# Gating two chunks a period sooner, and another order of the late block, in a retention + top-1 expert kernel on one Trainium2 core

## The chip, the core and the metric

The kernel runs on one core of a Trainium2 chip. Its engines work side by side and wait for each other by semaphores: TensorE (PE, with PEld for its weight loads), VectorE (DVE), ScalarE (ACT), GpSimd (POOL) and SyncE (SP, which issues most DMAs here; GpSimd issues the indirect ones). The metric is the device time of one execution in microseconds.

## What is computed

A retention (a decaying linear attention) over 4 batches of 768 positions, 8 heads of 64, gives 3072 rows of 512 numbers. Each row then goes through the one of 8 experts that its gate chooses, and is weighted by that gate's probability.

```python
for t in range(S):
    state = gamma * state + einsum('bhd,bhe->bhde', k[:, :, t], v[:, :, t])
    y[:, :, t] = scale * einsum('bhd,bhde->bhe', q[:, :, t], state)
...
logits = x @ w_gate
expert_idx = np.argmax(logits, axis=1)
...
for e in range(E):
    mask = expert_idx == e
    out[mask] = gate_w[mask, None] * (np.maximum(x[mask] @ w1[e], 0.0) @ w2[e])
```

## The kernel before

**Retention.** The 3072 rows are 24 chunks of 128, taken in 12 periods n = 0 to 11 of two chunks each (the loop `for n in range(last + 1)`). A period runs scores, state updates (`update` copies the state to a tile `ub` on ScalarE), outputs (`carry` reads `ub`, `output`), and `evict` writes the result xT. One period later `rows` transposes it to rows (`xrow`), and `logits` and `finish_logits` make gate logits.

**Gating.** Chunks are gated in groups, by the table `GROUPS` of (first chunk, count). A group is gated in the period after its last chunk: `choose` (VectorE: argmax, one-hot `EA`, shifted logits), `soft` (ScalarE: exp), `rank` (TensorE: small matmuls that count, for each row, the rows of the same expert ahead of it; one matmul for each earlier group's total among them), `slots` (VectorE: each row's slot, `KEY`), `weights`, `label` (ScalarE: weight and token number into `xrow`), `advance`. In the table of before, chunks 18 to 21 are one group, gated behind the loop; 22 and 23 follow.

**Scatter.** GpSimd sends each chunk's rows by an indirect DMA to their slots in `x_sorted` in DRAM, sorted by expert (`send_apart`, line 840). Between two sends stands `pause()`, a small operation (`idle`, line 201). After the last chunk come pads of zeros behind the regions.

**Expert 0's first 256 rows ("early").** Expert 0 is the class with the fewest rows among the first six chunks. Its first rows are read before the last period, and its matmuls (`early_pieces`, run by `fill`) fill TensorE from period 11 on, while the last chunks are gated and sent.

**Late block.** `late_block` takes up to 128 more rows of expert 0 (`xhl1`, read by SyncE as `xg1` after the last send). Its first layer is `hidden(i, part)` for weight halves i = 0, 1; ScalarE applies Relu (`hs`); `turned(i)` transposes on TensorE, ScalarE casts the high half of `hT` and VectorE subtracts for its low half (fp32 is carried as two fp32r numbers, high and low, so each product is three matmuls); `result(i, part)` is the second layer. In the same code the other engines prepare expert 1: its rows, read by SyncE into `buf`, are turned (VectorE), cast to `xh` (ScalarE) and subtracted to `xl` (VectorE) in four pieces by `prep(j, ...)`; the first part of its weights is split into `whi` (ScalarE) and `wlo` (VectorE) in two halves by `split(1, 0, i)`; `marks(1)` reads slot numbers. `weigh` (VectorE) scales the early results `Z0`, and `put_slices` (GpSimd) sends them to the output, eight indirect DMAs. The same buffers (tag "w", 11 of them, in turn) hold `Z0` and all weight halves.

**Experts 1 to 7** follow with all their rows each: eight column blocks of the first layer, then four of the second; weights are fetched by SyncE into two `raw` buffers, and split as they come free.

All this stands under a manual schedule: each engine runs its instructions in the order in which the code issues them.

Of the kernel before, what the change touches and what calls it, by code (L numbers as in the profile page):

```python
# [10 lines left out]
F32 = mybir.dt.float32  # L11
# [32 lines left out]
MAXB = CMAX32 // 32  # L44
WARM = 8
FILL = (1, 3, 4)
GROUPS = ((0, 6), (6, 6), (12, 4), (16, 2), (18, 4), (22, 2))
FULL = 18
BEHIND = {3: (0, 1), 4: (2, 3), 5: (4, 5), 6: (6, 7), 7: (10, 11), 8: (12, 13)}
AMID = {7: (8, 9)}  # L50
# [57 lines left out]
def retention_moe(ctx, tc, front, qkv, w1, w2, first_rows, second_rows, out):  # L108
# [112 lines left out]
    with ExitStack() as actx:  # L221
# [17 lines left out]
        def load(g, part=slice(0, 4)):  # L239
            if g not in qs:  # L240
                early = AHEAD <= g < FIRST or g in MID
                qs[g] = (wp.tile([P, 4, DM], F32, name="qkv_w", tag="w", bufs=11) if early else
                         ld.tile([P, 4, DM], F32, name="qkv_t", tag="ld"))
            nc.sync.dma_start(out=qs[g][:, part],
                              in_=front[2 * g + part.start // 2 - (g > 0)] if g <= AHEAD else qkv[g - AHEAD - 1])
# [22 lines left out]
        def bank(i, name, shape=(P, NP, C)):  # L268
            return ps_s.tile(list(shape), F32, name=name, tag=f"s{i}")
# [88 lines left out]
        def send_apart(chunks, between=pause):  # L358
            for i, g in enumerate(chunks):
                if i:  # L360
                    between()
                send_rows(g)
# [42 lines left out]
        def gating(i):  # L405
# [31 lines left out]
                nc.scalar.activation(out=ex[:, :, 0:E], in_=v["sh"], func=AF.Exp)  # L437

            def rank():
                pf = v["pf"] = bank(2, "pf", (P, NB, E)) if i < 3 else ps_1.tile([P, NB, E], F32, name="pf", tag="U" if i == 4 else "misc")  # L440
                nc.tensor.matmul(out=pf[:, 0:w, :], lhsT=us, rhs=Eb, start=True, stop=False, skip_group_check=True)
                for part in [run] + tots:
                    nc.tensor.matmul(out=pf, lhsT=ones, rhs=part.unsqueeze(1).broadcast_to([P, NB, E]),
                                     start=False, stop=False, skip_group_check=True)
                for n in range(NB - 1):
                    nc.tensor.matmul(out=pf[:, n + 1:, :], lhsT=ones,
                                     rhs=Eb[:, n:n + 1, :].broadcast_to([P, NB - 1 - n, E]),
                                     start=False, stop=(n == NB - 2), skip_group_check=True)
# [87 lines left out]
        def mark_early():  # L536
            xg0 = first["xg"]
            index, weight = slot_marks[0]
            empty = gsm.tile([P, NJ0], F32, name="empty0")
            nc.vector.tensor_tensor(out=empty, in0=k_("slot")[:, 0:NJ0], in1=s0.broadcast_to([P, NJ0]), op=ALU.is_ge)  # L540
            nc.vector.tensor_scalar(out=mask0, in0=empty, scalar1=float(BIG), scalar2=k_("quad"),
                                    op0=ALU.mult, op1=ALU.add)
            nc.vector.scalar_tensor_tensor(out=index[:, 0:NJ0], in0=xg0.bitcast(I32)[:, :, P], scalar=4 * ROWS,
                                           in1=mask0, op0=ALU.bitwise_and, op1=ALU.bitwise_or)
            nc.vector.tensor_copy(out=weight[:, 0:NJ0], in_=xg0[:, :, P + 1:P + 2])
# [60 lines left out]
        for n in range(last + 1):  # L606
# [95 lines left out]
            for g in (a, b):  # L702
                if FIRST <= g < NCH - AHEAD - len(MID):
                    load(g + AHEAD + len(MID))
                if g in fetches:
                    fetch(0, fetches[g])
                for i in LATER.get(g, ()):
                    load(i)
        mark_early()

        s = stages[4]
        fill(FILL[0])
        rows(2 * last, "U", ps_1)
        logits(last)
# [3 lines left out]
        s["rank"]()  # L718
        for name in ("slots", "weights", "advance", "label"):
            s[name]()  # L720
        send_apart(range(18, 22))
        finish_logits(last)
        final = gating(5)
        final["choose"]()
        fill(FILL[2])
        final["soft"]()
# [205 lines left out]
def moe_main(ctx, tc, wparts, fetch, split, xhl1, Z0, ident, buf, xg, fetch_rows, expert_at, held7, mask7, slot_marks, natural, overflow,  # L932
# [112 lines left out]
    def put_slices(e, j):  # L1045
        pause()
        scatter_rows(tc, out_slices, sidx[e][:, j:j + 1], Zs[e][:, j].rearrange("p k r -> p (k r)"), "rows")

    def late_block():

        hs = [yp.tile([P, DM], F32, name="hs", tag="yo") for _ in range(2)]
        hT = yp.tile([P, 2, KF, P], F32R, name="hT", tag="Z")
        hn = {}

        def hidden(i, part):
            whi, wlo = wparts[0, i]
            if part == 0:
                hn[i] = next(hidden_banks)
            for kd in range(2 * part, 2 * part + 2):
                for n, (a, x) in enumerate(((whi, 0), (wlo, 0), (whi, 1))):  # L1060
                    nc.tensor.matmul(out=hn[i], lhsT=xhl1[:, x, kd, :], rhs=a[:, kd, :],
                                     start=(kd == 0 and n == 0), stop=(kd == KD - 1 and n == 2))
            if part:
                nc.scalar.activation(out=hs[i], in_=hn[i], func=AF.Relu)

        def turned(i):
            t = next(hidden_banks).rearrange("p (j t) -> p j t", j=4)
            for j in range(4):
                nc.tensor.transpose(out=t[:, j, :], in_=hs[i][:, j * P:(j + 1) * P], identity=ident)
            hi, lo = [hT[:, n, 4 * i:4 * i + 4, :] for n in range(2)]  # L1070
            nc.scalar.copy(out=hi, in_=t)
            nc.vector.tensor_tensor(out=lo, in0=t, in1=hi.bitcast(F32), op=ALU.subtract)

        def result(i, part):
            whi, wlo = wparts[0, 2 + i]
            terms = ((whi, 0), (wlo, 0), (whi, 1))
            order = ([(f, n) for f in range(2 * part, 2 * part + 2) for n in range(3)] if i == 0 else
                     [(f, n) for f in range(4) for n in ((0, 1) if part == 0 else (2,))])
            for f, n in order:
                a, h = terms[n]  # L1080
                nc.tensor.matmul(out=pys[0], lhsT=hT[:, h, 4 * i + f, :], rhs=a[:, f, :],
                                 start=(i + f == 0 and n == 0), stop=(i == 1 and f == 3 and n == 2))

        prep = lambda j, *steps: prep_x(1, j, nc.vector, steps)
        for j in range(-(-NJ0 // 4)):
            weigh(0, j)
        for j in range(NJ0):
            put_slices(0, j)
        hidden(0, 0)
        hidden(0, 1)  # L1090
        prep(0, "turn")
        prep(1, "turn")
        prep(0, "high", "low")
        hidden(1, 0)
        turned(0)
        prep(1, "high")
        prep(2, "turn")
        hidden(1, 1)
        prep(1, "low")
        split(1, 0, 0, nc.vector)  # L1100
        result(0, 0)
        turned(1)
        prep(2, "high")
        split(1, 0, 1, nc.vector)
        prep(3, "turn")
        prep(2, "low")
        prep(3, "high", "low")
        marks(1)
        result(0, 1)
        result(1, 0)  # L1110
        result(1, 1)
        put_rows(0, pys[0], 0)

    with tc.manual_schedule():
# [238 lines left out]
```

## Time and profile before

| | us |
|---|---|
| time, median of 3 runs (lowest to highest) | 385.07 (384.97 to 385.78) |
| profiled execution | 385.23 |
| its span, first to last instruction | 383.5 |
| TensorE busy | 373.7 (97%) |
| VectorE busy | 251.6 (66%) |
| GpSimd busy | 263.5 (69%) |
| ScalarE busy | 140.4 (37%) |
| mean granted TensorE clock | 0.995 |

The views are all of one profiled execution, in microseconds from its first instruction. [...] The late block lies at 121 to 138, expert 1 behind it.

### The profile page before, as it was taken

The page shows a single profiled execution, that of the slowest core. Times are in us where ns is not written, and L with a number is a line of the kernel's source. Part 1 is how long each engine was busy: PE and PEld are TensorE (multiplying, and loading weights), DVE is VectorE, ACT ScalarE, POOL GpSimd, SP SyncE. Part 2 cuts the span into 40 slices and gives each one's busy share as a digit, 9 for nine tenths or more (in the row PEclk, how much of TensorE's full clock was granted, in tenths as well). Part 3 has the DMA queues.
Part 4 walks back from the last instruction along what each step waited for, and adds up shares of the span by engine and source line. Part 5 has one row for each costly group of instructions (what it writes and reads, how often), then busy time and mean ns, then how long its engine had stood idle before and what let it go on. Part 6 is the DMA issues. An engine that isn't in the chain of part 4 may idle for free. (4 is left out here: it accounts for less than half of the span.)

```text
span 383.5 us, 8677 instructions
## 1 busy us (share of the span) xinstructions
PE 373.7 (97%) x3272; PEld 350.5 (91%) x3272; DVE 251.6 (66%) x485; ACT 140.4 (37%) x248; POOL 263.5 (69%) x279
## 2 busy tenths in 40 slices
PE   7999999999999799999999999999999999999995
PEld 4888888788999589999999999999999999999984
DVE  3467758875787567877785778576766667676211
ACT  2222344245331446434441453154335416423100
POOL 3751669989380598005999799499759939986874
PEclk9999999999999899999999999999999999999999
DMA  8999999985037879769653773665466547530102
GB/s 305 416 414 420 415 399 419 414 339 170 32 140 149 287 183 252 243 222 249 215 216 78 190 234 141 131 220 159 154 174 194 201 83 233 181 125 17 37 29 76
DMA packets 42030, 82.05 MB, mean 214 GB/s; under 512 B 4267, under 2 KB 17583, under 8 KB 39536
## 3 DMA queue, kind: packets, MB, share of 16 engines
q1 hardware_dynamic: 36656, 67.67, 53.9%
q0 software_dynamic: 5312, 13.49, 9.8%
q8 instruction: 47, 0.77, 0.8%
q14 instruction: 15, 0.12, 0.1%
HBM read 65.80 MB, written 15.82 MB: 213 GB/s over the span
## 5 line engine op out<-in xcount | busy, mean ns | idle before, releaser
L840 POOL DMA_INDIRECT out<-Z,sidx x88 | 101.7, 1155 | 62.2 <-DVE Z L1043 47.4
L146 DVE TENSOR_TENSOR wlo<-raw,whi 128x1024 fp32r<-128x1024 f32 (+1 forms) x63 | 75.4, 1201 | 14.9 <-ACT whi L145 14.7
L201 POOL TENSOR_TENSOR idle<-cs 1x256 bf16<-1x256 f32 x103 | 82.5, 801 | 2.9
L145 ACT CAST whi<-raw 128x1024 fp32r<-128x1024 f32 (+1 forms) x72 | 67.5, 950 | 3.2 <-DMA raw<-w 3.2
L1201 PE MATMUL py<-hh,whi 128*128 128x392 f32 (+4 forms) x192 | 65.9, 343 | 0.0
L1201 PE MATMUL py<-hl,whi 128*128 128x392 f32 (+4 forms) x192 | 65.9, 343 | 0.0
L1201 PE MATMUL py<-hh,wlo 128*128 128x392 f32 (+4 forms) x192 | 65.9, 343 | 0.0
L1176 ACT ACTIVATE hh<-ph 128x452 fp32r<-128x452 f32 (+6 forms) x56 | 28.4, 507 | 76.9 <-PE ph L1169 75.2
L1169 PE MATMUL ph<-xh,whi 128*128 128x392 f32 (+5 forms) x224 | 48.9, 340 | 0.0
L1169 PE MATMUL ph<-xl,whi 128*128 128x392 f32 (+5 forms) x224 | 48.9, 340 | 0.0
L1169 PE MATMUL ph<-xh,wlo 128*128 128x392 f32 (+5 forms) x224 | 48.9, 340 | 0.0
L1177 DVE SCALAR_TENSOR_TENSOR hl<-ph,hh 128x452 fp32r<-128x452 f32 (+6 forms) x56 | 32.1, 574 | 20.8 <-ACT hh L1176 19.9
L1169 PEld LDWEIGHTS ph<-xh,whi 128*128 128x128 f32 x224 | 40.1, 188 | 0.7 <-ACT xh L862 0.5
L1169 PEld LDWEIGHTS ph<-xh,wlo 128*128 128x128 f32 x224 | 40.2, 188 | 0.1
L1169 PEld LDWEIGHTS ph<-xl,whi 128*128 128x128 f32 x224 | 40.2, 188 | 0.1
L1201 PEld LDWEIGHTS py<-hl,whi 128*128 128x128 f32 x192 | 36.1, 188 | 0.2
L1201 PEld LDWEIGHTS py<-hh,wlo 128*128 128x128 f32 x192 | 36.1, 188 | 0.2
L1201 PEld LDWEIGHTS py<-hh,whi 128*128 128x128 f32 x192 | 36.0, 188 | 0.2
L862 ACT CAST xh<-buf 128x512 fp32r<-128x512 f32 (+7 forms) x26 | 14.5, 556 | 58.2 <-DVE buf L855 58.2
L280 DVE TENSOR_TENSOR Sb<-sp,cs 128x512 f32<-128x512 f32 x48 | 29.9, 681 | 5.2 <-PE sp L277 5.2
L840 POOL DMA_INDIRECT x_sorted<-xrow,KEY x24 | 25.0, 1041 | 10.6 <-DVE mx L422 5.2
L1038 DVE STREAM_TRANSPOSE Z<-py 128x416 f32<-128x416 f32 (+3 forms) x24 | 15.0, 624 | 19.6 <-PE py L1201 19.4
(197 smaller groups left out, 552.0 us busy)
## 6 DMA issues: line engine op xcount, KB each, us to landing
raw<-w SPq DMA_DIRECT2D x32, 1024.0 KB, 6.7
qkv_w<-qkv SPq DMA_DIRECT2D x12, 1024.0 KB, 17.5
qkv_t<-qkv SPq DMA_DIRECT2D x7, 1024.0 KB, 16.4
qkv_t<-front SPq DMA_DIRECT2D x7, 512.0 KB, 6.8
buf<-x_sorted SPq DMA_DIRECT2D x12, 211.2 KB, 4.4
x_sorted<-cs SPq DMA_DIRECT2D x7, 260.0 KB, 5.7
buf<-x_sorted SPq DMA_DIRECT2D x8, 195.0 KB, 3.7
out<-Z,sidx POOLq DMA_INDIRECT x88, 2.8
```

The costliest lines, as they stand in the source:

```text
L145: nc.scalar.copy(out=hi[:, h], in_=raw[:, h])
L146: engine.tensor_tensor(out=lo[:, h], in0=raw[:, h], in1=hi[:, h].bitcast(F32), op=ALU.subtract)
L201: nc.gpsimd.tensor_tensor(out=idle[0:1], in0=cs[0:1, 0:PAUSE], in1=cs[0:1, 0:PAUSE], op=ALU.mult)
L280: nc.vector.tensor_tensor(out=Sb[:, r], in0=sps[r], in1=causal.unsqueeze(1).broadcast_to([P, NP, C]), op=ALU.mult)
L840: sc = tc.nc.gpsimd.indirect_dma_start(out=dst, out_offset=bass.IndirectOffsetOnAxis(ap=index, axis=0), in_=rows, in_offset=None, bounds_c ...
L862: nc.scalar.copy(out=xh[:, :, c0:c0 + w], in_=xt[:, :, t0:t0 + w])
L1038: nc.vector.transpose(out=Zs[e][:, 0:nb, k, :], in_=py[:, 0:32 * nb].rearrange("p (j c) -> p j c", c=32))
L1169: nc.tensor.matmul(out=ph[:, :w], lhsT=wparts[e, f // 4][a][:, kd, fo:fo + P], rhs=x[:, kd, :w], start=(n == 0), stop=(n == 3 * KD - 1))
L1176: nc.scalar.activation(out=hh[:, :cap], in_=ph[:, :cap], func=AF.Relu)
L1177: nc.vector.scalar_tensor_tensor(out=hl[:, :cap], in0=ph[:, :cap], scalar=0.0, in1=hh[:, :cap].bitcast(F32), op0=ALU.max, op1=ALU.subtract)
L1201: nc.tensor.matmul(out=py[:, :c], lhsT=a[:, f % 4, k * P:(k + 1) * P], rhs=x[:, :c], **se)
```

## The change

The table splits the group (18, 4) into (18, 2) and (20, 2). So chunks 18 and 19 are gated in period 10, in the loop, and sent by GpSimd behind the loop, ahead of everything that is gated there; chunks 20 and 21 are gated where 18 to 21 were. Which PSUM bank a rank uses is now chosen by the chunk number: 18's takes the bank of the earlier groups, 20's the one that 18's had.

In the late block the steps of VectorE and ScalarE stand in another order: the cast of `hT` ahead of the casts of routed rows, both weight halves behind all four pieces of rows, and the scaling and sending of the early results behind those. TensorE's order in the block is the same.

```diff
--- before.py
+++ after.py
@@ -44,7 +44,7 @@
 MAXB = CMAX32 // 32
 WARM = 8
 FILL = (1, 3, 4)
-GROUPS = ((0, 6), (6, 6), (12, 4), (16, 2), (18, 4), (22, 2))
+GROUPS = ((0, 6), (6, 6), (12, 4), (16, 2), (18, 2), (20, 2), (22, 2))
 FULL = 18
 BEHIND = {3: (0, 1), 4: (2, 3), 5: (4, 5), 6: (6, 7), 7: (10, 11), 8: (12, 13)}
 AMID = {7: (8, 9)}
@@ -437,7 +437,7 @@
                 nc.scalar.activation(out=ex[:, :, 0:E], in_=v["sh"], func=AF.Exp)
 
             def rank():
-                pf = v["pf"] = bank(2, "pf", (P, NB, E)) if i < 3 else ps_1.tile([P, NB, E], F32, name="pf", tag="U" if i == 4 else "misc")
+                pf = v["pf"] = bank(2, "pf", (P, NB, E)) if a < FULL - 2 or a == FULL else ps_1.tile([P, NB, E], F32, name="pf", tag="U" if a == FULL + 2 else "misc")
                 nc.tensor.matmul(out=pf[:, 0:w, :], lhsT=us, rhs=Eb, start=True, stop=False, skip_group_check=True)
                 for part in [run] + tots:
                     nc.tensor.matmul(out=pf, lhsT=ones, rhs=part.unsqueeze(1).broadcast_to([P, NB, E]),
@@ -706,9 +706,10 @@
                     fetch(0, fetches[g])
                 for i in LATER.get(g, ()):
                     load(i)
+        send_apart(range(FULL, FULL + 2))
         mark_early()
 
-        s = stages[4]
+        s = stages[5]
         fill(FILL[0])
         rows(2 * last, "U", ps_1)
         logits(last)
@@ -718,9 +719,9 @@
         s["rank"]()
         for name in ("slots", "weights", "advance", "label"):
             s[name]()
-        send_apart(range(18, 22))
+        send_apart(range(20, 22))
         finish_logits(last)
-        final = gating(5)
+        final = gating(6)
         final["choose"]()
         fill(FILL[2])
         final["soft"]()
@@ -1082,33 +1083,32 @@
                                  start=(i + f == 0 and n == 0), stop=(i == 1 and f == 3 and n == 2))
 
         prep = lambda j, *steps: prep_x(1, j, nc.vector, steps)
-        for j in range(-(-NJ0 // 4)):
-            weigh(0, j)
-        for j in range(NJ0):
-            put_slices(0, j)
         hidden(0, 0)
         hidden(0, 1)
         prep(0, "turn")
         prep(1, "turn")
-        prep(0, "high", "low")
         hidden(1, 0)
         turned(0)
-        prep(1, "high")
+        prep(0, "high", "low")
         prep(2, "turn")
         hidden(1, 1)
-        prep(1, "low")
-        split(1, 0, 0, nc.vector)
+        prep(1, "high", "low")
+        prep(3, "turn")
         result(0, 0)
+        prep(2, "high")
         turned(1)
-        prep(2, "high")
-        split(1, 0, 1, nc.vector)
-        prep(3, "turn")
         prep(2, "low")
         prep(3, "high", "low")
+        for i in range(2):
+            split(1, 0, i, nc.vector)
         marks(1)
+        for j in range(-(-NJ0 // 4)):
+            weigh(0, j)
         result(0, 1)
         result(1, 0)
         result(1, 1)
+        for j in range(NJ0):
+            put_slices(0, j)
         put_rows(0, pys[0], 0)
 
     with tc.manual_schedule():
```

On GpSimd, from the last weight half inside the loop to the third send (`x_sorted<-xrow,KEY` is the send of a chunk, `idle` the pause; in brackets the semaphores that the instruction waits for: of VectorE, ScalarE, GpSimd, or of DMAs). Before:

```order
L146 TENSOR_TENSOR wlo<-raw,whi 128x512 [waits Activation_49]
L840 DMA x_sorted<-xrow,KEY 25600x520 [waits DMAHW3_49,DMAHW4_49,DMAHW2_49,DMAHW5_49,DMASW2_49,DMAHW6_49,DVE_49,Activation_49]
L201 TENSOR_TENSOR idle<-cs 1x256
L840 DMA x_sorted<-xrow,KEY 25600x520 [waits DMASW3_49]
L201 TENSOR_TENSOR idle<-cs 1x256 [waits Pool_49]
L840 DMA x_sorted<-xrow,KEY 25600x520 [waits DMASW4_49]
```

and now:

```order
L146 TENSOR_TENSOR wlo<-raw,whi 128x512 [waits Activation_49]
L841 DMA x_sorted<-xrow,KEY 25600x520 [waits DMAHW4_49,DMAHW5_49,DMAHW3_49,DMAHW6_49,DMAHW2_49,DMASW2_49]
L201 TENSOR_TENSOR idle<-cs 1x256
L841 DMA x_sorted<-xrow,KEY 25600x520 [waits DMASW3_49]
L841 DMA x_sorted<-xrow,KEY 25600x520 [waits DMASW4_49,DVE_49,Activation_49]
L201 TENSOR_TENSOR idle<-cs 1x256 [waits Pool_49]
```

The sends are the same in number and order, but the first two (18 and 19) wait for no other engine any more, only for DMAs that were issued long before; it is the third (20) that waits for VectorE and ScalarE, and no pause stands ahead of it.

On ScalarE, from the cast of the late rows to the first Relu of expert 1 (`hs`, `hT` are of the late block, `xh<-buf` are routed rows of expert 1, `whi` its weights). Before:

```order
L862 CAST xhl_1900<-xt_1902 128x512
L1064 ACTIVATE hs<-ph_2169 128x512
L862 CAST xh<-buf 128x4x128
L1071 CAST hT<-ph_2171 128x512
L862 CAST xh<-buf 128x4x128
L1064 ACTIVATE hs<-ph_2170 128x512
L145 CAST whi<-raw 128x1024
L1071 CAST hT<-ph_2169 128x512
L862 CAST xh<-buf 128x4x128
L145 CAST whi<-raw 128x1024
L862 CAST xh<-buf 128x4x68
```

and now:

```order
L863 CAST xhl_1924<-xt_1926 128x512
L1065 ACTIVATE hs<-ph_2193 128x512
L1072 CAST hT<-ph_2195 128x512
L863 CAST xh<-buf 128x4x128
L1065 ACTIVATE hs<-ph_2194 128x512
L863 CAST xh<-buf 128x4x128 x2
L1072 CAST hT<-ph_2193 128x512
L863 CAST xh<-buf 128x4x68
L145 CAST whi<-raw 128x1024 x2
```

The first `hT` moved ahead of the first `xh`, the second behind three of them, and both weight halves to the end.

On VectorE, from the turns of the early results `Z` to the slot numbers of expert 1 (`buf<-buf` are turns of routed rows, `xl` their low halves, `hT` the low halves of the late block, `wlo` the weights'). Before:

```order
L1043 TENSOR_TENSOR Z_2127<-Z_2127,gw_105 128x512 x2
L855 STREAM_TRANSPOSE buf<-buf 128x4x4x32 x2
L869 TENSOR_TENSOR xl<-buf,xh 128x4x128
L1072 TENSOR_TENSOR hT<-ph_2171,hT 128x512
L855 STREAM_TRANSPOSE buf<-buf 128x4x4x32
L869 TENSOR_TENSOR xl<-buf,xh 128x4x128
L146 TENSOR_TENSOR wlo<-raw,whi 128x1024
L1072 TENSOR_TENSOR hT<-ph_2169,hT 128x512
L146 TENSOR_TENSOR wlo<-raw,whi 128x1024
L855 STREAM_TRANSPOSE buf<-buf 128x3x4x32
L869 TENSOR_TENSOR xl<-buf,xh 128x4x128
L869 TENSOR_TENSOR xl<-buf,xh 128x4x68
```

and now:

```order
L856 STREAM_TRANSPOSE buf<-buf 128x4x4x32 x2
L1073 TENSOR_TENSOR hT<-ph_2195,hT 128x512
L870 TENSOR_TENSOR xl<-buf,xh 128x4x128
L856 STREAM_TRANSPOSE buf<-buf 128x4x4x32
L870 TENSOR_TENSOR xl<-buf,xh 128x4x128
L856 STREAM_TRANSPOSE buf<-buf 128x3x4x32
L1073 TENSOR_TENSOR hT<-ph_2193,hT 128x512
L870 TENSOR_TENSOR xl<-buf,xh 128x4x128
L870 TENSOR_TENSOR xl<-buf,xh 128x4x68
L146 TENSOR_TENSOR wlo<-raw,whi 128x1024 x2
```

The low half of `hT` stands behind two turns of routed rows and ahead of their first low half; the two weight halves went behind all rows, and the scaling of `Z` left this place (it follows the slot numbers).

Besides, in period 10 TensorE has seven more small matmuls (the rank of 18 and 19) between the outputs and the state update of chunk 22; VectorE chooses for these chunks ahead of evicting the period's outputs; and on ScalarE the copy of that state, `ub`, stands behind the two label copies.

## Rows read from the trace of the kernel before

**Rows 1.** Part 1 of the page: busy us (share of the span) xinstructions, whole span.

```profile
PE 373.7 (97%) x3272; PEld 350.5 (91%) x3272; DVE 251.6 (66%) x485; ACT 140.4 (37%) x248; POOL 263.5 (69%) x279
```

**Rows 2.** Who TensorE waited for, 60:160: us in total, times, longest us.

```profile
PE py L1081 <- ACT hT L1071: 2.1, 1, 2.1
```

**Rows 3.** Stretches: length, busy us (xinstructions) by engine, granted clock, DMA share, GB/s.

```profile
121.24:127.55 6.31, 6.31 (x30) 4.64 (x28) 3.30 (x10) 0.60 (x1) 0.00 (x0) 1.00 1.17 234
127.55:129.63 2.08, 0.00 (x0) 0.00 (x0) 1.81 (x3) 1.15 (x3) 1.16 (x2) 1.00 1.06 392
129.63:133.60 3.97, 3.93 (x11) 2.86 (x12) 3.54 (x5) 2.07 (x4) 3.62 (x4) 0.57 0.74 281
133.60:137.75 4.15, 4.14 (x18) 3.00 (x17) 2.92 (x5) 2.31 (x4) 3.77 (x5) 1.00 0.10 32
```

**Rows 4.** Timeline of TensorE, late block: start us, us, instruction, idle before it.

```profile
125.55 0.60 PE L1069 MATMUL ph<-cs,hs 128*128 128x128 f32 x4
125.90 0.48 PE L1061 MATMUL ph<-whi,xhl 128*128 128x512 f32 x1
...
129.63 0.51 PE L1081 MATMUL py<-whi,hT 128*128 128x512 f32 x1 [2.08 <-ACT hT L1071]
...
137.75 1.03 PE L1169 MATMUL ph<-xh,whi 128*128 128x420 f32 x4
```

**Rows 5.** Timeline of ScalarE, late block.

```profile
128.48 0.62 ACT L862 CAST xh<-buf 128x512 fp32r<-128x512 f32 x1 [3.54 <-DVE buf L855]
129.00 0.58 ACT L1071 CAST hT<-ph 128x512 fp32r<-128x512 f32 x1
```

**Rows 6.** Timeline of VectorE, late block.

```profile
127.73 1.31 DVE L855 STREAM_TRANSPOSE buf<-buf 128x512 f32<-128x512 f32 x2 [3.14 <-DMA buf<-x_sorted]
...
129.74 0.68 DVE L1072 TENSOR_TENSOR hT<-ph,hT 128x512 fp32r<-128x512 f32 x1
...
131.57 1.61 DVE L146 TENSOR_TENSOR wlo<-raw,whi 128x1024 fp32r<-128x1024 f32 x1
...
135.52 1.23 DVE L146 TENSOR_TENSOR wlo<-raw,whi 128x1024 fp32r<-128x1024 f32 x1 [0.78 <-ACT whi L145]
...
137.16 1.01 DVE L869 TENSOR_TENSOR xl<-buf,xh 128x512 fp32r<-128x512 f32 x2
```

**Rows 7.** Timeline of GpSimd, sends of sorted chunks 18, 19 and 23.

```profile
102.94 1.01 POOL L840 DMA_INDIRECT x_sorted<-xrow,KEY  x1 [5.21 <-DVE mx L422]
...
104.75 1.01 POOL L840 DMA_INDIRECT x_sorted<-xrow,KEY  x1 [0.16 <-issue]
...
112.77 1.01 POOL L840 DMA_INDIRECT x_sorted<-xrow,KEY  x1 [0.16 <-issue]
```

**Rows 8.** Timeline of SyncE, read of expert 1's rows.

```profile
119.00 1.91 SPq L155 DMA_DIRECT2D buf<-x_sorted  x4
```

**Rows 9.** Timeline of ScalarE (label of 22, 23) and of VectorE (pad slots).

```profile
105.67 0.20 ACT L491 CAST xrow<-cs 128x8 int32<-128x8 f32 x1
...
109.35 0.23 DVE L371 TENSOR_SCALAR pads<-ends,cs 128x7 int32<-128x7 f32 x1
```

**Rows 10.** Timeline of TensorE, sixth period: rank, state update, use of the state.

```profile
56.78 0.20 PE L441 MATMUL pf<-EA,us 128*128 128x48 bf16 x1
...
57.07 0.69 PE L292 MATMUL U<-vs,qkv_w 128*64 128x64 f32 x16
...
60.16 0.62 PE L314 MATMUL Y<-qkv_t,ub 64*64 64x128 f32 x16
```

**Rows 11.** Timeline of ScalarE, sixth period (state copy) and expert 1 (weight half).

```profile
59.42 0.36 ACT L295 COPY ub<-U 128x256 f32<-128x256 f32 x1
...
161.08 1.05 ACT L145 CAST whi<-raw 128x1024 fp32r<-128x1024 f32 x1
```

**Rows 12.** Line 840, 131:152: ns min/median/max, first and last start; landing us.

```profile
L840 POOL DMA_INDIRECT out<-Z,sidx x8: 1007/1009/1803, 132.3 to 148.3; - x8
...
DMA to landing us min/median/max: 3.1/4.4/5.2
```

## Prediction

> **What bounds the kernel now.** I read the share of busy time first: TensorE is busy for 97% of the span, the next engine for 69% [rows 1]. So a change pays only where TensorE stands still or runs slowly, and the second view, who waited for whom on TensorE, says where: from 60 us on it has one long wait, 2.1 us for the cast of hT in the late block [rows 2], and after 160 us none at all. [...] The hole is paid twice, once idle and once at half speed behind it.
>
> Why the hole: the timelines of the other engines [rows 4 to 6]. TensorE's four transposes for the first half of hT ended at 125.55 + 0.60 = 126.15, but ScalarE cast them at 129.00 only, straight behind a cast of routed rows (xh<-buf at 128.48). That one needs VectorE's turn, which began at 127.73, when expert 1's rows had landed. VectorE's low half of hT stands behind those rows too (129.74). So the late block, which needs none of these rows, waits for their transfer.
>
> Why the rows are late: the queues ahead [rows 7, 8]. GpSimd sits idle for 5.21 us until 102.94, then sends chunks 18 to 23 one by one, 104.75 - 102.94 = 1.81 us apart where nothing slows it; 23 goes at 112.77, the first pad behind it. SyncE, which has waited for that send, then reads the late rows and, from 119.00, expert 1's, which are used 8.7 us after that.
>
> **Part 1: chunks 18 and 19 a period sooner.** Two sends leave the chain: they go into the idle 5.21 us (2 x 1.81 = 3.6 us fit). Chunk 20 still waits for its label, so it goes near 103.2; then 21 at 105.0, 22 at 106.8, 23 at 108.6, the pad at 110.4. What 22 and the pad need is there: the label of 22 is cast by 105.87, the pad slots are written at 109.58 [rows 9], each up to 0.3 us later now. Chunk 23 is thus sent 4.2 us sooner, and since SyncE's two reads, the value load between them and the weight fetch behind them keep their order, I move them by the same 4.2 us: expert 1's rows are read at 114.8 and usable at 123.5. The same traffic surrounds that read as before, so I keep its 8.7 us.
>
> What it adds is a rank of 7 small matmuls in period 10, in the same place as that of group 1 in period 6: there 8 such matmuls took 57.07 - 56.78 = 0.29 us [rows 10]. I take 0.29; the bounds are 0 (the tail loses one such matmul and gains one, so it gives nothing back) and 0.7 us, if a wait joins. The candidates for a wait: VectorE's choice must be done before the rank, and the state copy ub stands on ScalarE behind the label copies, which wait for VectorE. In period 6 ub ended at 59.42 + 0.36 = 59.78 [rows 11], its reader on TensorE began at 60.16, 0.38 us later, and no wait shows [rows 10]. Period 10 has the same order with a third of the elements, so I book none. VectorE does a dozen small operations there that stood behind the loop; work of the same kind made no wait in period 6.
>
> **Part 2: the order in the late block.** On ScalarE the first hT cast now stands ahead of every routed row, so the rows can't hold it. On VectorE two turns of rows still precede the low half of hT. The first two result matmuls need only the cast, the third needs the low half.
>
> With rows at 123.5, VectorE ends both turns at 124.9 (1.31 us) and is free when the cast comes (near 127.0); the low half ends near 127.7 (0.68 us). TensorE gets there at 127.55 + 0.29 = 127.84 and finds both. The cover is 2.5 us: rows may land up to 126.0 before TensorE waits. With no hole I book no fall of the clock: every stretch here that has none shows 1.00 [rows 3].
>
> What is late next is expert 1's first layer. From 127.84 the block has 24 result matmuls and four transposes. At full clock a result matmul comes every 4.15 / 18 = 0.23 us [rows 3] and four transposes cost 125.90 - 125.55 = 0.35 [rows 4]. So the block ends at 127.84 + 5.53 + 0.35 = 133.7, where it ended at 137.75. Expert 1 then needs xh and the high weight halves at once and the low weight halves some 0.8 us later. The change puts both weight halves of VectorE last: behind the second low half of hT (the cast comes near 130.3) stand 0.68 us of it, two low halves of rows (1.01 together) and two weight halves of 1.23: 130.3 + 4.2 = 134.5 [rows 6]. TensorE wants them at 134.5 and 134.8. This fits without cover; if a half takes 1.61 as one did, TensorE waits 0.1 to 0.4 us.
>
> The scaling of Z (1.27 us) and the eight sends of finished slices go behind all this. GpSimd had begun them at 132.3, the last at 148.3 [rows 12]; now they begin near 135.3, the last near 151.4. I cost this at nothing: GpSimd had time behind them, and the buffer of Z is wanted again only by the high weight half that ScalarE cast at 161.08 [rows 11], 157.1 now.
>
> **The sum.** Expert 1 starts at 133.7 instead of 137.75: 2.08 of the hole, 2.2 of slow clock and waits behind it, less 0.29 for the rank, 4.0 us in all. Behind it TensorE had no wait to the end, and weights are fetched as buffers come free, so the gain should arrive whole. The profiled execution took 385.23 us (span 383.5), the median 385.07; 4.0 off gives 381.2 and 381.1. I say 381.2.
>
> **The rivals.**
> (a) The rows land hardly sooner, because their transfer, not the sends, sets 127.7 (for it: 8.7 us from issue to use is long; against it: they were issued right behind the late rows' read, which follows send 23). Then VectorE's low half of hT ends at 127.73 + 1.31 + 0.68 = 129.7, TensorE does two matmuls and stands from 128.3 to 129.8, the clock falls again, and VectorE's list puts the last weight half near 137.1. Expert 1 starts near 137.3: 0.4 us gained, 384.8. In between, each us that rows land after 126.0 costs one, and about one more once the clock falls. [...]
> (b) The rank in period 10 does make TensorE wait, for the choice or for ub behind the labels. For it: the margin of ub in period 6 is only 0.38 us. Price: 0.5 to 1.5 us, so 381.7 to 382.7.
> (c) Slower: the slice sends are late. The first high half of the weights from the buffer of Z must wait until all eight slices have left it, and behind it on ScalarE stand the casts of expert 2's rows. If the last slice lands after 157.1, the wait begins, and at worst each us of it is lost at the start of expert 2. I expect it at 151.4 + 4.4 = 155.8 [rows 12]. To lose the 4.0 us and 0.8 more, it would have to land at 161.9, 6 us later: 386.0. Slices that meet the weight fetches may take 1 or 2 us longer, so this is unlikely.
> (d) It doesn't do what it says: VectorE's choice or the labels for 18 and 19 are late, so GpSimd holds these two and the rest with them, and the rows come as before: again 384.8. Against: both are written inside period 10, which is over when GpSimd's idle begins at 102.94 - 5.21 = 97.73.
>
> **How the numbers follow.** The forecast, 3.4 to 4.4 us gained (380.7 to 381.7): 0.66. (b): 0.09. (a) in part, gains of 0.8 to 3.3 us: 0.11. (a) whole or (d), within 0.8 us: 0.07. (c) or another wait that turns it over: 0.07. The range for 8 in 10 takes the forecast, (b) and the better part of (a): 380.6 to 383.0. A difference of 0.2% (0.77 us) is about the least that a measurement of this kernel tells from none; faster by more than that 0.86, within it 0.07, slower 0.07.
>
> **What would show it.** Right: chunk 23 sent near 108.6, expert 1's rows first turned near 123.7, no wait of TensorE on hT, the granted clock 1.00 through the block, expert 1's first matmul near 133.8, and the shift kept to the end. Wrong, part 1: the first turn of rows still after 126. Part 2: a wait on the low half of hT or on the low weight halves at expert 1's start. (b): a wait of TensorE between 88 and 93 us. (c): a wait of TensorE after 160 us, on xh of expert 2 or on weights.

## The result: 381.4 us, and where the 3.6 us came from

| | before | changed |
|---|---|---|
| time, median | 385.02 us (384.6 to 385.78) | 381.42 us (381.2 to 381.46) |
| ratio | | 0.9892, 95% interval 0.9875 to 0.9909 |
| span of the profiled execution | 383.5 us, clock 0.995 | 379.6 us, clock 0.998 |
| TensorE busy | 373.7 us | 372.5 us |

381.2 was forecast, with 380.6 to 383.0 as range. Two more groups of runs had the changed kernel beside the kernel before: 381.35 against 385.36 (0.990) and 382.95 against 386.87 (0.9903). The ratios are those on record with their intervals, not quotients of the medians (here 381.42 / 385.02 = 0.9906, inside the interval); by the ratio the gain is 4.2 us, by the medians 3.6.

The place that bounded the kernel first: TensorE in the late block, changed kernel (start, duration, engine, line, operation, count; in brackets idle time ahead and what ended it). It answers to [rows 4].

```profile
126.12 0.60 PE L1070 MATMUL ph<-cs,hs 128*128 128x128 f32 x4
126.47 0.48 PE L1062 MATMUL ph<-whi,xhl 128*128 128x512 f32 x1
...
127.72 0.39 PE L1062 MATMUL ph<-whi,xhl 128*128 128x512 f32 x1
127.95 0.39 PE L1082 MATMUL py<-whi,hT 128*128 128x512 f32 x1
128.18 0.40 PE L1082 MATMUL py<-wlo,hT 128*128 128x512 f32 x1
128.42 0.62 PE L1082 MATMUL py<-whi,hT 128*128 128x512 f32 x2
...
133.08 1.09 PE L1082 MATMUL py<-whi,hT 128*128 128x512 f32 x4
134.01 0.93 PE L1169 MATMUL ph<-xh,whi 128*128 128x420 f32 x4
```

The bracket with 2.08 is gone: the first result matmul follows the last one of the first layer by 0.23 us. The same stretch in the table of stretches (length, busy time of TensorE, its weight loads, VectorE, ScalarE and GpSimd, granted clock of TensorE as a share of full speed, DMA share, GB/s) has no idle time, and the clock is 1.00 where [rows 3] had 0.57:

```profile
127.80:133.90 6.10, 6.10 (x30) 4.95 (x29) 6.03 (x10) 4.66 (x8) 0.00 (x0) 1.00 0.10 38
```

Why, on ScalarE and VectorE of the changed kernel (compare [rows 5, 6]):

```profile
126.81 0.59 ACT L1072 CAST hT<-ph 128x512 fp32r<-128x512 f32 x1 [1.30 <-PE ph L1070]
127.29 0.62 ACT L863 CAST xh<-buf 128x512 fp32r<-128x512 f32 x1
...
123.84 1.26 DVE L856 STREAM_TRANSPOSE buf<-buf 128x512 f32<-128x512 f32 x2
127.43 0.69 DVE L1073 TENSOR_TENSOR hT<-ph,hT 128x512 fp32r<-128x512 f32 x1 [2.33 <-ACT hT L1072]
...
132.20 2.35 DVE L146 TENSOR_TENSOR wlo<-raw,whi 128x1024 fp32r<-128x1024 f32 x2
```

ScalarE now waits for TensorE's transposes and VectorE for ScalarE's cast of them, neither of them for rows. VectorE turned the rows at 123.84, straight behind its work of before, so they had landed by then; it then stood 2.33 us until hT came. And why the rows are early, on GpSimd and in SyncE's queue (compare [rows 7, 8]):

```profile
98.70 1.29 POOL L841 DMA_INDIRECT x_sorted<-xrow,KEY  x1
...
100.78 1.01 POOL L841 DMA_INDIRECT x_sorted<-xrow,KEY  x1 [0.16 <-issue]
103.48 0.97 POOL L841 DMA_INDIRECT x_sorted<-xrow,KEY  x1 [1.69 <-ACT xrow L491]
...
108.84 1.04 POOL L841 DMA_INDIRECT x_sorted<-xrow,KEY  x1 [0.16 <-issue]
...
110.69 1.27 POOL L841 DMA_INDIRECT x_sorted<-cs,pads  x1 [0.16 <-issue]
...
115.11 1.91 SPq L155 DMA_DIRECT2D buf<-x_sorted  x4
```

**The account.** One mark ahead of all that the change touches is the first U of period 10 on TensorE (86.32 before, 86.53 now). From there to the last matmul of the block's first layer (127.16, 127.72), from that to expert 1's first matmul (137.75, 134.01), and from that to the end. The first two marks before, then the first one now:

```profile
86.32 0.69 PE L292 MATMUL U<-vs,qkv_t 128*64 128x64 f32 x16
...
127.16 0.39 PE L1061 MATMUL ph<-whi,xhl 128*128 128x512 f32 x1
...
86.53 0.69 PE L292 MATMUL U<-vs,qkv_t 128*64 128x64 f32 x16
```

| TensorE, us | before | changed | difference |
|---|---|---|---|
| to the first U of period 10 | 86.32 | 86.53 | +0.21 |
| to the block's last first-layer matmul | 40.84 | 41.19 | +0.35 |
| to expert 1's first matmul | 10.59 | 6.29 | -4.30 |
| to the end of the span | 245.75 | 245.59 | -0.16 |
| span | 383.5 | 379.6 | -3.9 |

The marks matter below too. In the traces of the two groups of runs whose kernel before took 386.9 us, that U stands at 87.4 to 88.2, and in the group with 385.4 at 86.3 to 88.1, whatever the kernel: 1 to 2 us are lost ahead of all that is studied here. So across groups the stretches are compared, or the ratio.

### The profile page after: what moved, and what is told of

It is laid out like the page before. It is cut to its first block, busy times and chain, and to the rows that moved or that the text cites. A ratio compares the mean times of both kernels' runs of the same rounds, so it can differ in the third digit from the quotient of the medians.

```text
span 379.6 us, 8704 instructions
## 1 busy us (share of the span) xinstructions
PE 372.5 (98%) x3279; PEld 350.5 (92%) x3279; DVE 251.9 (66%) x495; ACT 140.6 (37%) x251; POOL 262.2 (69%) x278
## 5 line engine op out<-in xcount | busy, mean ns | idle before, releaser
L146 DVE TENSOR_TENSOR wlo<-raw,whi 128x1024 fp32r<-128x1024 f32 (+1 forms) x63 | 74.2, 1184 | 17.5 <-ACT whi L145 17.4
L201 POOL TENSOR_TENSOR idle<-cs 1x256 bf16<-1x256 f32 x102 | 80.4, 788 | 2.9
```

The lines of the kernel that those rows point to most:

```text
L146: engine.tensor_tensor(out=lo[:, h], in0=raw[:, h], in1=hi[:, h].bitcast(F32), op=ALU.subtract)
L201: nc.gpsimd.tensor_tensor(out=idle[0:1], in0=cs[0:1, 0:PAUSE], in1=cs[0:1, 0:PAUSE], op=ALU.mult)
```

## Experiments

**Each part alone.** Part 1 alone has the groups and sends of the changed kernel and the late block of the kernel before; part 2 alone the reverse. Against the kernel before, cut to the core, first part 1, then part 2:

```diff
-GROUPS = ((0, 6), (6, 6), (12, 4), (16, 2), (18, 4), (22, 2))
+GROUPS = ((0, 6), (6, 6), (12, 4), (16, 2), (18, 2), (20, 2), (22, 2))
...
+        send_apart(range(FULL, FULL + 2))
         mark_early()
...
-        send_apart(range(18, 22))
+        send_apart(range(20, 22))
```

```diff
-        prep(0, "high", "low")
         hidden(1, 0)
         turned(0)
+        prep(0, "high", "low")
...
+        for i in range(2):
+            split(1, 0, i, nc.vector)
         marks(1)
```

> Part 1 alone: the groups split and chunks 18 and 19 sent at the retention's end, the late block in the order of the kernel before. Theory A (the time at which the routed rows land decides; the order in the block is a help of small size): chunk 23 goes at 108.8 and the rows are there near 123.1 as in the changed kernel; on VectorE the scaling of Z (1.27 us) now stands ahead of their turns, which run from 124.6 to 125.9; ScalarE cuts the first piece at 125.3, long before the transposes for hT end near 126.7, so TensorE finds hT and its low half, there is no hole and the clock stays at 1.00; 381.2 to 381.8 us. Theory B (the order decides, since ScalarE and VectorE take their work in the order written): a wait on hT of at least 1 us is left, 382.9 us or more.

> Part 2 alone: groups and sends of the kernel before, the late block in the new order. Theory A: the rows are turned from 127.7 to 129.0 as before; the cast of hT goes at 126.3 now, but VectorE's low half of it stands behind the turns and ends at 129.7; TensorE does two result matmuls, stands from about 128.0 to 129.8 and runs slowly behind that; little or nothing is gained, 384.3 to 385.4 us. Theory B: the order decides, most of the 4 us is gained, 381 to 382.5 us.

Part 1 alone: 383.36 us, ratio 0.9914 (0.9884 to 0.9944). As a time that lies in the range of theory B, but the kernel before took 386.93 in this group, and the changed kernel with three more pauses (below), which waits for nothing, 382.97; so the trace decides. TensorE and ScalarE of part 1 alone, and the stretch:

```profile
129.32 0.39 PE L1062 MATMUL ph<-whi,xhl 128*128 128x512 f32 x1
...
135.90 1.03 PE L1170 MATMUL ph<-xh,whi 128*128 128x420 f32 x4
...
135.42 0.42 ACT L863 CAST xh<-buf 128x272 fp32r<-128x272 f32 x1 [1.78 <-DVE buf L856]
```

```profile
129.50:135.85 6.35, 6.26 (x29) 4.72 (x28) 5.76 (x8) 4.03 (x7) 5.78 (x7) 1.00 0.13 43
```

There is no wait on hT, and the stretch to expert 1 is 6.58 us: 4.0 of the 4.3 us. Theory A holds. What the old order keeps is 0.3 us at the end, since expert 1's last rows come last there: their cast ends at 135.84, 0.06 us ahead of expert 1's first matmul. The weight halves were done by then (the second wlo, begun at 133.67, took 1.23 us).

Part 2 alone: 385.04 us, ratio 0.9969 (0.9947 to 0.9992), a gain of about 1.2 us by the ratio, where none or little was expected. By itself that time says little: the kernel with the additional rank alone, which should gain nothing, has the same ratio in this group (below). ScalarE, VectorE and TensorE of part 2 alone, and then the stretch behind the hole:

```profile
128.23 0.59 ACT L1071 CAST hT<-ph 128x512 fp32r<-128x512 f32 x1 [1.30 <-PE ph L1069]
...
129.28 1.30 DVE L855 STREAM_TRANSPOSE buf<-buf 128x512 f32<-128x512 f32 x2 [3.87 <-DMA buf<-x_sorted]
130.51 0.65 DVE L1072 TENSOR_TENSOR hT<-ph,hT 128x512 fp32r<-128x512 f32 x1
...
129.62 0.39 PE L1081 MATMUL py<-wlo,hT 128*128 128x512 f32 x1
131.22 0.73 PE L1081 MATMUL py<-whi,hT 128*128 128x512 f32 x2 [1.21 <-DVE hT L1072]
```

```profile
131.20:136.00 4.80, 4.78 (x22) 3.78 (x23) 4.73 (x8) 3.43 (x6) 2.56 (x3) 1.00 0.70 262
```

The mechanism is the expected one: the wait has moved from ScalarE's cast to VectorE's low half, behind the turns. But the hole is 1.21 us, and the clock behind it stayed at 1.00. The stretch to expert 1 is 7.85 us, 2.74 less than before. Of that, some 0.44 us is this execution's own: its rows were turned 0.13 us after the block's last first-layer matmul, in the kernel before 0.57 us after it. One execution of either kernel was traced.

**Rows later, order kept.** Three, six and nine more pauses ahead of the pad:

```diff
-        pause()
+        for _ in range(4):   # 7, 10
+            pause()
         sent = send_pad(1)
```

> The changed kernel with three more pauses on GpSimd (0.6 us each and 0.16 between) ahead of the pad behind which expert 1's rows are read: these rows, and the weight fetches behind them, come 2.3 us later, near 125.4, and nothing else moves. If the low half of hT is what is late first, the turns (1.26 us) end at 126.7, ahead of the cast of hT (127.4), and TensorE waits for nothing: 381.4 us, as the changed kernel, within 0.3. If the cover is smaller than the 2.5 us that the prediction gave, TensorE waits on hT or on expert 1's weights: 382 us or more.

> The changed kernel with six more pauses ahead of the pad: expert 1's rows 4.6 us later, about where the kernel before has them. Theory A (the low half of hT stands behind the turns; the cover is 2.5 us): TensorE stands for about 1.2 to 1.8 us ahead of the third result matmul, as with part 2 alone, and expert 1 starts that much later, plus whatever the clock costs behind it; if the clock keeps 1.00, as it did behind the 1.21 us hole of part 2 alone, 1.5 us more than the changed kernel; if it falls as in the kernel before, 3 to 3.5 us more. Theory B (the order in the block takes the rows off the path altogether): no wait and the time of the changed kernel.

> Nine more pauses: expert 1's rows 6.8 us later, 2.3 us behind those of the kernel before. Theory A: a hole of 3.5 to 4 us ahead of the third result matmul, with the clock fallen behind it: 5 to 6.5 us more than the changed kernel, that is 1.5 to 3 us slower than the kernel before. If the idle time alone counts and the clock does not fall: 3.5 to 4 us more. Theory B: no wait, or one on expert 1's own rows only, less than 2 us more.

> The changed kernel once more, beside the others of this call, since the first four kernels ran where the kernel before took 386.9 us instead of 385.0. It should stand to the kernel before as it did: 3.6 us less, and with the block of the late rows (last matmul of its first layer to last group of its second) at 5.36 us as in its first trace.

With three, 382.97 us beside a kernel before of 386.93 (0.9905, as the changed kernel): no wait. With six, 383.30 us, 1.95 more than the changed kernel beside it (381.35); from the U of period 10 to the end it is 1.1 more (294.24 against 293.13). With nine, 384.67 us, 3.3 more, and 3.7 from the U on (296.86). The pauses moved the rows less than planned: the read followed the pad by 4.4 us in the repeat of the changed kernel (110.54 to 114.98) and by 3.0 with nine pauses (118.00 to 120.96), so part of them went into slack. Against the U of period 10 the first turn came 1.55, 3.30 and 4.70 us later. VectorE with three pauses, then TensorE with six and with nine, each with the stretch behind its hole:

```profile
126.63 1.30 DVE L857 STREAM_TRANSPOSE buf<-buf 128x512 f32<-128x512 f32 x2 [1.26 <-DMA buf<-x_sorted]
128.86 0.69 DVE L1074 TENSOR_TENSOR hT<-ph,hT 128x512 fp32r<-128x512 f32 x1 [0.93 <-ACT hT L1073]
```

```profile
130.60 0.73 PE L1083 MATMUL py<-whi,hT 128*128 128x512 f32 x2 [0.49 <-DVE hT L1074]
```

```profile
130.60:135.40 4.80, 4.80 (x22) 3.78 (x23) 4.73 (x8) 3.43 (x6) 2.55 (x3) 1.00 0.70 263
```

```profile
130.29 0.81 PE L1083 MATMUL py<-whi,hT 128*128 128x512 f32 x2 [1.83 <-DVE hT L1074]
```

```profile
130.29:134.30 4.01, 4.01 (x13) 3.23 (x14) 3.65 (x6) 2.51 (x5) 2.54 (x3) 0.57 1.02 381
```

So theory A holds here as well, and its price has two steps. The 0.49 us hole cost 0.87 us (block 7.13 against 6.26 us), that is 0.38 beyond its idle time; the 1.21 us hole of part 2 alone cost 1.59 (7.85 against 6.26), again 0.38 beyond; the 1.83 us hole was followed by 4 us at 0.57, and the block took 9.94 us, 3.7 more, 1.85 beyond its idle time. For the 2.08 us of the kernel before it is 1.93 beyond (10.59 against the 6.58 of part 1 alone, which has the same order and no hole). My estimates for six pauses (a hole of 1.2 to 1.8 us) and for nine were too high because the rows moved 3.3 us and not 4.6, and 4.7 and not 6.8. The repeat of the changed kernel came out as expected: 6.26 us in the block, 4.0 us less than the kernel before.

**The additional rank alone.** Groups split, but GpSimd held until the weights of 20 and 21 are there, old order in the block:

```diff
-        send_apart(range(20, 22))
+        nc.gpsimd.tensor_copy(out=idle[:, 0:2], in_=GW[:, 20:22, 0])
+        send_apart(range(18, 22))
```

> The group split alone: chunks 18 and 19 are gated in period 10, but GpSimd holds their sends until the weights of 20 and 21 are there (one copy of 2 columns that reads them), and the late block has the old order. This is the price of the additional rank. If the rank costs what its 7 matmuls take: 0.3 us, TensorE's carry of period 10 later by 0.3, 385.3 us beside 385.0, too little for the time and enough for the trace. If a wait joins it (the rival b of the prediction): 0.6 us or more, with a wait of TensorE between 88 and 93 us, 385.7 us or more.

The time was a miss: 385.56 us, ratio 0.9966 (0.9949 to 0.9983), less than the kernel before. Its trace shows no gain: from the U of period 10 to the end 297.64 us, the kernel before 297.18 in its own trace. The hole was 1.43 us here and the clock behind it 0.67, where the kernel before had 2.08 and 0.57:

```profile
130.92:135.90 4.98, 4.87 (x15) 3.65 (x16) 4.23 (x6) 3.79 (x6) 4.60 (x5) 0.67 0.73 272
```

The traced execution is the slowest of this kernel's eleven (386.74 us). In it the block came later against expert 1's rows: they were turned 0.08 us ahead of the block's last first-layer matmul, before 0.57 us after it, which is the 0.65 us by which the hole is shorter. The stretch to expert 1 is 9.92 us, 3.34 more than in part 1 alone and so 1.91 beyond the idle time. No trace of the kernel before was taken in that group of runs, so why the median fell stays open. For the rank the trace will do. On TensorE of the changed kernel, period 10 (the load of `us` is on the weight-load row):

```profile
88.90 0.18 PE L441 MATMUL pf<-EA,us 128*128 128x16 bf16 x1
88.94 0.17 PE L443 MATMUL pf<-run,ones 128*128 128x16 bf16 x1
88.97 0.24 PE L443 MATMUL pf<-tot,ones 128*128 128x16 bf16 x4
89.07 0.17 PE L446 MATMUL pf<-EA,ones 128*128 128x8 bf16 x1
89.16 0.69 PE L292 MATMUL U<-vs,qkv_t 128*64 128x64 f32 x16
...
88.90 0.10 PEld L441 LDWEIGHTS <-us 128*128 128x128 bf16 x1 [0.17 <-issue]
...
91.36 0.36 ACT L295 COPY ub<-U 128x256 f32<-128x256 f32 x1
...
91.76 1.10 PE L314 MATMUL Y<-qkv_t,ub 64*64 64x128 f32 x32
```

The seven matmuls take 89.16 - 88.90 = 0.26 us. The group of Y ahead of them takes 1.85 us to the next start (87.05 to 88.90) where it took 1.74 (86.84 to 88.58), and the weight load of `us` has 0.17 us of idle time ahead of it there. From the second U to the carry it is 2.60 us instead of 2.56. Together 0.41. The last two lines are the place of rival (b): the copy ub ends at 91.36 + 0.36 = 91.72, only 0.04 us ahead of its reader, and in the kernel before it was done 1.45 us ahead (89.69, 91.14). It is 0.03 to 0.05 us in every trace with the rank. From the scores to the carry TensorE takes 1.98 or 1.99 us in all of them, as without the rank, so no wait came of it. Over all traces, from U to the block's last first-layer matmul, it is 40.71 to 40.91 us without the rank (three kernels) and 41.19 to 41.40 with it (eight); three with another loss in that stretch are left out, the one above, where VectorE waited 0.50 us for the late rows, and two below.

**Early rows without the rank.** Old groups, but no pauses between the sends of 18 to 23 and the pad:

```diff
-        send_apart(range(18, 22))
+        send_apart(range(18, 22), lambda: None)
...
-        pause()
-        send_apart(range(22, 24))
+        send_apart(range(22, 24), lambda: None)
...
-        pause()
         sent = send_pad(1)
```

> The new order of the block, but the groups of the kernel before (18 to 21 gated together, no rank in period 10), and the pauses between the sends of 18 to 23 and ahead of the pad taken out (six of them, 0.76 us each with the issue). If a send holds GpSimd for the 1.0 us of its record, the sends follow each other at about 1.05 us, chunk 23 goes 3.8 us sooner than in the kernel before, expert 1's rows land about where the changed kernel has them, there is no hole, and the time is 0.3 us less than that of the changed kernel, since the rank is gone. If the sends are slower where they follow each other directly (1.3 to 1.8 us apart), the rows come only 1 to 2.5 us sooner than before, TensorE waits up to 1 us for the low half of hT, and the time is 0.5 to 2 us more than that of the changed kernel.

> The version without the pauses and without the additional rank, in more rounds. In its first trace, from the first U of period 10 to the end of the span, it took 292.65 us where the changed kernel took 293.07 and 293.13. If that is the rank, the time is 0.4 us less than the changed kernel's; if the first run was luck, the two are equal within 0.2.

> The changed kernel, as the measure for the three others of this call: 381.4 us where the kernel before takes 385.0, 3.6 us apart.

> No pauses, old groups and the old order of the late block: three lines beside the kernel before. It shows what part 2 is worth once the rows are early. Theory A (the time at which the rows land decides): no hole, block of 5.36 us, clock 1.00, expert 1 some 0.3 us later than with the new order because its last piece of rows and its second weight half come later, so 0.3 us more than the version without pauses in the new order. Theory B (the order is needed too): a wait on hT and 2 us more or worse.

In the first run the sends stood 1.28 us apart, not 1.05, which was enough: no hole, 381.19 us beside 381.35 of the changed kernel, and 0.5 us less from the U on (292.65). The same kernel in the next group took 387.84 us in the median (387.29 to 388.91), 4.9 more than the changed kernel beside it, and slower than the kernel before (1.003, interval 1.0016 to 1.0043). With the old order 389.14 us, 1.3 more, where 0.3 was expected; 1.1 of it is lost ahead of the block's last first-layer matmul. In the traces of that group TensorE stands in the early pieces, ahead of the late block. GpSimd, TensorE, ScalarE and VectorE, without pauses, second group, and two stretches there:

```profile
110.83 0.97 POOL L838 DMA_INDIRECT x_sorted<-xrow,KEY  x1 [0.30 <-issue]
...
112.11 0.97 POOL L838 DMA_INDIRECT x_sorted<-cs,pads  x1 [0.31 <-issue]
...
111.60 0.28 PE L893 MATMUL ph<-xh,wlo 128*128 128x256 f32 x1 [0.68 <-issue]
...
113.03 0.51 PE L893 MATMUL ph<-xl,whi 128*128 128x256 f32 x3 [1.03 <-issue]
...
115.02 0.41 PE L916 MATMUL acc<-hh,whi 128*128 128x256 f32 x1 [1.48 <-ACT hh L901]
...
114.59 0.38 ACT L901 ACTIVATE hh<-ph 128x256 fp32r<-128x256 f32 x1 [7.12 <-PE ph L893]
...
115.00 0.42 DVE L902 SCALAR_TENSOR_TENSOR hl<-ph,hh 128x256 fp32r<-128x256 f32 x1 [4.25 <-ACT hh L901]
```

```profile
110.91:115.00 4.09, 0.92 (x6) 0.68 (x4) 0.00 (x0) 0.41 (x2) 1.86 (x2) 1.00 0.57 202
115.00:120.30 5.30, 5.28 (x31) 5.14 (x32) 2.67 (x6) 2.23 (x6) 0.00 (x0) 0.68 0.69 132
```

"issue" means that the profile shows nothing it waited for. The third gap waits for ScalarE's hh, which began 1.05 us after the matmul ahead of it ended; VectorE stood because it waits for hh in its turn. 0.92 us of matmuls in 4.09, then 5.3 us at a clock of 0.68 (0.50 with the old order). It came in both kernels without pauses that were traced in that group, within 0.1 us at the same place, but neither in the changed kernel nor in that of the next section, traced beside them, nor in the first run of the same kernel. The two kernels that stall also have the old groups, so that the missing pauses are the cause is likely (the kernel before has the old groups and took 386.87 us in this group) but not shown; nor is what they would space out. So this is no improvement, and the one that I looked for beyond the changed kernel was not found. For the order it still answers the question: with early rows (the block came some 5 us later, so they were there in any case) the stretch to expert 1 is 6.26 us in the new order and 6.57 in the old, 0.3 us as with part 1 alone; theory A holds.

**The finished slices.** Scaling and sends back to the front of the block, against the changed kernel:

```diff
+        for j in range(-(-NJ0 // 4)):
+            weigh(0, j)
+        for j in range(NJ0):
+            put_slices(0, j)
         hidden(0, 0)
...
-        for j in range(-(-NJ0 // 4)):
-            weigh(0, j)
         result(0, 1)
         result(1, 0)
         result(1, 1)
-        for j in range(NJ0):
-            put_slices(0, j)
```

> The changed kernel with the scaling of Z and the eight sends of finished slices put back to the front of the block. The prediction cost their move at nothing. If so: the sends run from about 127 to 143, the turns of rows begin 1.3 us later, still ahead of the cast of hT, and the time is that of the changed kernel within 0.2. If moving them gained something (their transfers no longer beside expert 1's weights): 0.3 to 0.8 us more than the changed kernel. If the late slices cost something at the start of expert 2: 0.3 us less or better.

383.63 us beside 382.95 of the changed kernel: 0.68 more, which is what was expected if the move gained something. But up to expert 1's first matmul nothing differs (47.61 us from the U, against 47.67), with the eight sends from 129.17 to 145.25. Most of the rest falls in one place, the start of the second column of expert 1's result:

```profile
158.36 0.35 PE L1201 MATMUL py<-hl,whi 128*128 128x420 f32 x1
159.04 0.45 PE L1201 MATMUL py<-hh,whi 128*128 128x420 f32 x1 [0.33 <-issue]
```

0.68 us from one matmul to the next instead of 0.20. A branch on the number of rows stands there. The two intervals (0.9901 to 0.9936, and 0.9886 to 0.9921) overlap, and part 2 alone had 0.21 us of the same kind there with the new order, so that the old place of the slices causes it is not shown. A gain by moving them is likely small, 0 to 0.7 us, and I had booked none.

## Why the prediction was right, point by point

- **The bound.** Right. The hole at hT and the slow clock behind it (0.57 over the 3.97 us of [rows 3], 0.50 from 130.2 to 133.2 us in the same trace) were booked at 2.08 + 2.2 = 4.28 us, and the stretch lost 4.30.
- **Part 1.** Right. Chunk 23 went at 108.84 (forecast 108.6), the read of the rows at 115.11 (114.8), the first turn at 123.84 (123.5), where VectorE had only just become free. Every one of these is some 0.3 us late, about what the mark (0.21) and the part of the rank that was not booked (0.12) add up to. GpSimd's next pad, which waits for the same read, went at 123.16, so the rows were there by then. Part 1 alone brought 4.0 us of the 4.3.
- **The rank.** The mechanism right, the size short: 0.29 booked, 0.41 at its place. Rival (b), a wait for the choice or for ub, did not come, but that was luck: period 6, from which I took it, has 0.38 us between ub and its reader, period 10 has 0.04. The surplus lies in the seams on both sides of the seven matmuls. A price per matmul from period 6 didn't have them.
- **Part 2, the cover.** Booked at 2.5 us, rows until 126.0. Right: the turns take 1.3 us and the low half 0.65, the third result matmul is due at 128.42, so turns may begin until about 126.4; 1.55 us later cost nothing, and 3.30 and 4.70 us later left 0.49 and 1.83 us of idle time, so the cover measured is 2.8 and 2.9 us.
- **The weight halves last.** Right: done at 132.20 + 2.35 = 134.55 (forecast 134.5) without a wait of TensorE. What I had not seen is that the order also spares 0.3 us at expert 1's start against part 1 alone.
- **Rival (a), rows late in the new order.** Its mechanism is what part 2 alone and the runs with more pauses show: a wait on the low half. In the trace of part 2 alone the cast of hT ended at 128.82, VectorE stood idle until 129.28 for the rows, and the low half followed their turns at 130.51. (The 129.74 of the kernel before, which the prediction cites, shows less: there the cast itself ended only at 129.58.) Its price was too high: 0.4 us of gain left, where part 2 alone gained about 1.2 us by the ratio and 2.7 in the stretch. Two steps of that rival failed: "the clock falls again", which I took for certain (1.00 behind the 1.21 us hole of the one execution traced), and expert 1's start behind the last weight half (it started at 137.00, that half was done at 135.64 + 2.35 = 137.99).
- **Rival (c), slices late.** Sends from 135.60 to 150.36 (forecast 135.3 to 151.4), and TensorE waits for nothing after 160 us. Their raw neighbours got later: a high weight half at 149.11 waited 2.87 us for its transfer, where the longest such wait between 138 and 162 us was 1.02 us before. TensorE did not notice.
- **Rival (d).** It did what it says: 18 left at 98.70, 19 at 100.78.
- **The sum.** 4.0 booked. The span lost 3.9 (4.30 + 0.16 less 0.35 and 0.21, the last of them ahead of period 10), the median 3.6 in this group of runs and 4.0 and 3.9 in the two others.

## What to carry over

When an engine holds work for the critical engine behind a transfer, as VectorE did in part 2 alone (idle for rows from 128.82 to 129.28, with the cast for the low half of hT done), ask which of two edits pays: bring the transfer forward, or move the work ahead of it. Here the first alone was worth 4.0 us and the second alone 2.7 in the stretch that counts, but together 4.3, because they take away the same hole. Price an idle gap of TensorE by the stretch behind it, not by its length alone (here 0.4 us beyond the idle time where the clock stayed, 1.9 where it fell), and before taking out a spacing that looks idle, run it more than once: back-to-back sends were even with the changed kernel in one group of runs and 4.9 us slower in the next.

## What the runs showed that I had not expected

- **A hole is not always paid twice.** Idle times of 0.49 and 1.21 us were followed by a granted clock of 1.00; 1.43 us by 0.67; 1.83 and 2.08 us by 0.57 for 4 us. Against the same order without a hole, the first two cost 0.38 us beyond their idle time, the other three 1.91, 1.85 and 1.93, much the same whatever their length. Each is one execution. I had seen only the 2.08 and its clock.
- **A stall of TensorE beside sends without pauses**, with ScalarE and VectorE waiting for its products: most of 4.1 us (0.92 us of matmuls in 110.91 to 115.00), in one group of runs and not in another, cause not shown.
- **A small stall at the start of a result column**, 0.33 us with the slices in front and 0.21 in part 2 alone, with "issue" ahead of it, comes and goes between kernels whose TensorE does the same there. A branch stands there, but no run shows what TensorE waits for: with the slices in front no packet of the two instruction queues (q8 and q14 in the view of the DMAs) falls between 156 and 162 us, and the stall lies at 158.7 to 159.0.
